# A linear-attention and mixture-of-experts kernel: ScalarE's order in the first steps, an earlier load of the experts' first rows, and the last tile scaled by two engines

## The chip, the cores and the metric

The kernel runs on one core of a Trainium2 chip. The core has five engines with their own instruction queues: TensorE (PE, matmuls; PEld are its weight loads), VectorE (DVE), ScalarE (ACT), GpSimd (POOL) and SyncE (SP, which here only issues DMA transfers). They run in parallel and meet at semaphores. The metric is the device time of one execution in microseconds (us), the median of several.

## The reference, cut to what matters

```python
f = 1.0 / (1.0 + np.exp(-f_logit))              # batch 4, heads 8, seq 768, head_dim 48
for t in range(S):
    state = f[:, :, t, :, None] * state + np.einsum('bhd,bhe->bhde', k[:, :, t], v[:, :, t])
    y[:, :, t] = np.einsum('bhd,bhde->bhe', q[:, :, t], state)
x = y.transpose(0, 2, 1, 3).reshape(B * S, H * D)   # 3072 tokens of 384 numbers
logits = x @ w_gate                              # 8 experts
expert_idx = np.argmax(logits, axis=1)
gate_w = softmax(logits)[expert_idx]
h = np.maximum(x_of_expert @ w1[e], 0.0)         # 384 -> 1024
y = h @ w2[e]                                    # 1024 -> 384
out = gate_w[:, None] * y
```

First a gated linear attention, then a layer in which each token goes to the one expert with the largest logit. How many tokens an expert gets is known only when all tokens have been through the attention.

## The kernel before, in words

**First half, attention in units.** The sequence is cut into 6 chunks of 128 tokens and the batch into two pairs, which gives 12 units (`NU`). The recurrence inside a unit becomes matmuls: with the running sum of log f, keys are multiplied by its exponential (`growth`, `by_r`) and queries by its inverse (`decay`, `by_decay`). For each unit, `steps` and `log` compute exp and log of f on ScalarE, `total` is VectorE's running sum, `score` is q times k (PE s), `mask` copies the causal half out of PSUM (VectorE, 4 per unit), `keys` transposes k on TensorE into PSUM (kp) and `keep` copies it to SBUF on ScalarE (kn), `within` and `before` make the output (PE yt), `added` and `update` make the new state (PE dp), `settle` copies yt to ys on ScalarE. `rows` turns ys into token rows and logits by matmuls (PE xp), and `lay` copies these rows out of PSUM on ScalarE into xr. `turns` gives out two PSUM buffers in turn to kp, xp, dp and a few others, so dp of a step needs the buffer of the first xp, which has to be copied out by `lay` before.

**The order.** It is written out by hand: the loop over `n` from 1 to 13 (`NU + 1`) issues the instructions of step n for units n+3 to n-2, and every engine executes its own in this order. Unit n's scores, unit n-1's outputs and unit n-2's rows fall into step n. `settle(last)` stands at the head of a step and copies unit n-2's output. There is one yt buffer in PSUM and one ys buffer in SBUF.

**Routing.** When a group of units (0 and 1, 2 and 3, ... , 10, 11) has its rows, `choose` (six small VectorE operations) finds each token's expert, `count` ranks the tokens by two matmuls, `place` turns this into a row of the DRAM buffer `xs`, `fill` writes the gate weight, and `send` scatters the rows by indirect DMA from GpSimd (L183), 128 tokens per scatter, 24 in all. Up to units 4 and 5 a step sends two scatters; later groups send all of theirs at once. The scatters are declared not to depend on each other, but a load from xs waits for all scatters ahead of it in the program, and a scatter behind a load waits until the load has landed.

**Early experts.** Experts 0 and 1 (`EARLY`) start before all tokens are placed. Their first 128 rows are loaded at the end of step 11:

```python
            if n == NU - 1:
                soon = [load_rows(first[e]) for e in range(EARLY)]
```

Each `load_rows` is four transfers of 48 KB and one small one (tg: token and gate). VectorE transposes them (`turn`), and TensorE widens them (L304 into s) in between the last attention steps, then narrows them (L320 into yp). In `settled`, three tiny VectorE operations (L716 to L720) test whether these experts have 128 rows at the time when they are loaded; if not, a slow path at the end repairs it. Weights of experts 0 and 1 (two tensors of 1.5 MB each) are loaded at the ends of steps 8 and 10.

**Second half, the experts.** For each expert, in tiles of up to 384 rows: `widen` (PE hps, L304), relu on ScalarE and VectorE in turn, `narrow` (PE yps, L320) for each 128 rows, and `put`: VectorE multiplies by the gate weight (L331) and GpSimd scatters the rows into the output.

Of the kernel before, what the change touches and what calls it, by code (L numbers as in the profile page):

```python
# [10 lines left out]
F32 = mybir.dt.float32  # L11
# [108 lines left out]
def kernel(  # L120
# [194 lines left out]
                else:  # L315
                    nc.vector.tensor_scalar(to, x["h"], 0.0, None, op0=OP.max)  # L316

    def narrow(x, t, w, yp, group="out"):
        for f in range(NF):
            nc.tensor.matmul(  # L320
                yp,
                lhsT=x["hT"][:, f, t * C : t * C + C],
                rhs=w[1][:, f, :],
                start=f == 0,
                stop=f == NF - 1,
            )
        put(x, t, yp, group)

    def put(x, t, yp, group):
        ysb = ep.tile([128, DM], F32, name="ysb")  # L330
        nc.vector.tensor_scalar(ysb, yp, x["tg"][:, t, 1:2], None, op0=OP.mult)  # L331
        scatter(out, x["dst"][:, t : t + 1], ysb, N - 1, group)


# [48 lines left out]
    with ExitStack() as st:  # L383
# [92 lines left out]
        def ends(u):  # L476
            nc.gpsimd.tensor_copy(rend[:, u], units[u]["sum"][:, :, C])

        def decay(u, part=whole):
            x = units[u]  # L480
            x["dec"] = x["g"][:, :, 1:CR]
            nc.scalar.activation(
                x["dec"][:, part], x["sum"][:, part, 1:CR], AF.Exp, scale=-1.0
            )
# [223 lines left out]
        def settled(n, rt):  # L708

            rt.place()  # L710
            rt.fill()
            lead["base"] = rt.after
            if n == NU - 3:
                lack = wk.tile([1, EARLY], F32, name="lack", bufs=1)
                some = wk.tile([1, 1], F32, name="some", bufs=1)
                nc.vector.tensor_tensor(  # L716
                    lack, rt.after[0:1, 0:EARLY], const("full")[0:1, 0:EARLY], op=OP.is_lt
                )
                nc.vector.reduce_max(some, lack, axis=AX_X)
                nc.vector.tensor_copy(fix, some)  # L720
            if n < NU:
                for c in range(0, rt.n, 2):
                    sends.append(lambda c=c: rt.send(range(c, c + 2)))
            else:
                rt.send(range(rt.n))
# [3 lines left out]
        def scatter_some(n):  # L729
            now = sends if n >= NU - 1 else sends[:1]  # L730
            for send in now:
                send()
            del sends[: len(now)]
# [31 lines left out]
        for n in range(1, NU + 2):  # L765
            here, back, last = n, n - 1, n - 2
            ahead = n + 1 < NU
            state = n < NU - 2
            rt = None
            if here < NU:  # L770
                units[here]["old"] = states[here % 2]
            if 1 <= last:
                settle(last)
            if later and later[0] < NU - 1:
                later[1].weigh()
            if here < NU:
                for a in range(2):
                    score(here, a)
            if ahead and n != 2:
                by_r(n + 1)  # L780
                ends(n + 1)
            if decayed:
                decayed()
                decayed = None
            if sends:
                scatter_some(n)
            if n == 1:
                units[0]["old"] = None
                added(0)
                update(0)()  # L790
            if ahead and n != 2:
                decay(n + 1)
                last_decay(n + 1)
            if state:
                keys(here)
                keep(here)
            if n == 2:
                growth(n + 1)
                by_r(n + 1)
                ends(n + 1)  # L800
                decay(n + 1)
                last_decay(n + 1)
            if here < NU:
                for a in range(2):
                    for h in range(2):
                        mask(here, a, h)
            if n == 1:
                log(3)
            if n + 3 < NU:
                steps(n + 3)  # L810
            if later and n >= NU - 1:
                settled(*later)
                later = None
                scatter_some(NU)
            if 2 < n < NU - 2:
                total(n + 2)
            if n == NU - 2:
                by_decay(n + 1)
            if 0 <= last:
                rt = rows(last, later[1] if later else None)  # L820
                lay(last)
            if later and n == NU - 2:
                settled(*later)
                later = None
                scatter_some(NU)
            if ahead and n < NU - 2:
                by_decay(n + 1)
            if n == 2:
                total(n + 2)
            if rt:  # L830
                rt.choose()
                if n < NU - 2:
                    routed.append(rt.latest)
                if n >= NU - 1:
                    rt.weigh()
            if later:
                settled(*later)
                routed.append(later[1].latest)
                later = None
            for a in range(2):  # L840
                if back < NU:
                    within(back, a)
            if n == 1:
                settle(0)
            if n + 2 < NU and n != 1:
                growth(n + 2)
            if n == NU + 1:
                widen(soon[0], weights[0], early_h, range(3, 7))
            if n == NU:
                turn_early(soon[0])  # L850
            if state:
                added(here)
                decayed = update(here)
            if n == 1:
                total(3)
            if back < NU:
                before(back)
            if rt:
                later = (n, rt)
                if n >= NU - 1:  # L860
                    rt.count(turns("rp", [128, 2, rt.n, E]))
                if n >= NU:
                    settled(*later)
                    later = None
            if n == NU:
                early_h = early_banks()
                widen(soon[0], weights[0], early_h, range(3))
            if n == NU + 1:
                widen(soon[0], weights[0], early_h, range(7, NF))
                turn(soon[1])  # L870
            if n == 1:
                load(n + 3, "q")
            if n + 3 < NU:
                load(n + 3, "k")
            if n + 2 < NU:
                load(n + 2, "v")
            if 1 < n and n + 3 < NU:
                load(n + 3, "q")
            if n + 5 < NU:
                load(n + 5, "f")  # L880
            if n == 1:
                load_first_pads()
            if n in (8, 10):
                load_first_weights((n - 8) // 2)
                load_second_weights((n - 8) // 2)
            if n == NU - 1:
                soon = [load_rows(first[e]) for e in range(EARLY)]


        def share():  # L890
# [91 lines left out]
    def tile_pools(st):  # L982
        pool = lambda name, bufs: st.enter_context(tc.tile_pool(name=name, bufs=bufs, space=PSUM))
        psh, psz = pool("psh", 6), pool("psz", 2)

        def bank(i):
            return psh.tile([128, 512], F32, name="hps")

        def narrow_late(x, t, w, group="out"):
            narrow(x, t, w, psz.tile([128, DM], F32, name="yps"), group)  # L990

        return bank, narrow_late, psz

    with ExitStack() as st:
# [86 lines left out]
        for e in range(E):  # L1081
            x, w = rows_of[e], weights[e]
            x["hT"] = qp.tile([128, NF, TILES * C], F32, name="hT")[:, :, 0 : x["n"] * C]
            widen(x, w, bank, range(NF))
            if e in WITH:
                widen_quad(quad)
            if e + 1 < E:
                turn(rows_of[e + 1])
            if e + 1 in WITH:
                turn(quad, qp)  # L1090
            if e + 2 < E:
                rows_of[e + 2] = load_expert(e + 2)
                load_first_weights(e + 2)
            fetch(2 * e)
            if e in WITH:
                turn_quad(quad)
            for t in range(x["n"]):
                if e in WITH and t == 2:
                    narrow_quad(quad)
                narrow_late(x, t, w)  # L1100
            if e + 2 < E:
                load_second_weights(e + 2)
            fetch(2 * e + 1)
# [155 lines left out]
```

## Time and profile before

| | us |
|---|---|
| time, median of 3 | 409.92 |
| lowest and highest | 407.5, 410.32 |
| span of the profiled execution | 410.9 |
| TensorE busy | 390.1 |
| VectorE, GpSimd, ScalarE busy | 170.6, 112.3, 102.9 |

A line of the profile names the engine, the source line, the operation, the output and its inputs, and a count. An idle time in brackets stands before an instruction with the work that ended it; "issue" means that the profile shows nothing it waited for, and "remote" a semaphore whose sender is not in the records. The chain of work that ended last is followed back from the last instruction, at each step to what released it. The attention ends near 127 us; the experts fill the rest.

### The profile page before, as it was taken

Reading aid. Unit: us, or ns where it says so; the run is one execution under the profiler, and the core shown is the slowest. Engines: PE = TensorE matmul, PEld = TensorE weight load, DVE = VectorE, ACT = ScalarE, POOL = GpSimd, SP = SyncE. Lnnn points to the kernel's source line nnn. Section 1 sums busy time; section 2 is a strip of 40 time slices with the busy share of each in tenths; the row PEclk is TensorE's granted clock in tenths of the full one; section 3 lists DMA queues with packets and bytes.
Section 4 is the critical chain, followed back from the end, with each engine's and each line's share of the span. In section 5 each row is a group of like instructions: output and inputs, shape, how many; then the busy total and the mean of one; then the engine's idle time right before and its main releaser. Section 6 shows DMA issues by size and latency. Waiting matters only on the chain.

```text
span 410.9 us, 7299 instructions
## 1 busy us (share of the span) xinstructions
PE 390.1 (95%) x2870; PEld 272.1 (66%) x2870; DVE 170.6 (42%) x364; ACT 102.9 (25%) x190; POOL 112.3 (27%) x118
## 2 busy tenths in 40 slices
PE   7878999999999699999999999999999999999991
PEld 7878899989978478685555555545455555554540
DVE  6989888887752631212131131119112113111810
ACT  7888778675232001010100100110000000001000
POOL 5378667778705200000001001000200100100020
PEclk9998999999999699999999999999999999999997
DMA  8998667769953358785539999892172379994010
GB/s 291 406 359 296 213 213 256 237 200 360 404 156 105 121 157 282 176 294 109 185 108 396 362 384 332 322 352 31 51 255 83 97 252 383 405 406 169 1 46 17
DMA packets 52122, 95.22 MB, mean 232 GB/s; under 512 B 21440, under 2 KB 41333, under 8 KB 50032
## 3 DMA queue, kind: packets, MB, share of 16 engines
q1 hardware_dynamic: 48592, 84.96, 61.1%
q0 software_dynamic: 3200, 9.64, 6.3%
q8 instruction: 24, 0.39, 0.4%
q10 hardware_dynamic: 288, 0.08, 0.1%
q14 instruction: 18, 0.15, 0.1%
HBM read 79.65 MB, written 15.40 MB: 231 GB/s over the span
## 4 chain that ended last, share of the span: by engine, by line
PE 86%; DMA 4%; ACT 3%; DVE 2%; another core or an unknown queue 1%; issue 1%; SPq 0%; POOL 0%; POOLq 0%; ACTq 0%; DVEq 0%
PE yps L320 28%; PE hps L304 28%; PE xp L625 6%; PE yt L533 5%; PE s L505 4%; DMA f<-in_fu_dram 4%; PE yp L320 3%; PE yps L1059 3%; PE hps L1033 3%; PE yt L554 2%; PE s L304 2%; PE dp L570 2%; PE kp L520 1%; ACT g L438 1%
## 5 line engine op out<-in xcount | busy, mean ns | idle before, releaser
L320 PE MATMUL yps<-w2t,hT 128*128 128x384 f32 x352 | 115.6, 487 | 0.0
L304 PE MATMUL hps<-xT,w1t 128*128 128x384 f32 (+1 forms) x384 | 114.9, 459 | 0.0
L304 PEld LDWEIGHTS hps<-xT,w1t 128*128 128x128 f32 x384 | 73.0, 190 | 41.1
L320 PEld LDWEIGHTS yps<-w2t,hT 128*128 128x128 f32 x352 | 66.5, 190 | 48.1 <-issue 2.9
L183 POOL DMA_INDIRECT out_dram<-ysb,dst x26 | 25.3, 972 | 239.7 <-DVE ysb L331 239.4
L314 ACT ACTIVATE hT<-hps 128x384 f32<-128x384 f32 (+1 forms) x28 | 14.1, 505 | 209.7 <-PE hps L304 190.8
L316 DVE TENSOR_SCALAR hT<-hps 128x384 f32<-128x384 f32 (+1 forms) x28 | 16.2, 577 | 97.2 <-PE hps L304 97.2
L331 DVE TENSOR_SCALAR ysb<-yps,tg 128x384 f32<-128x384 f32 x22 | 13.6, 618 | 73.4 <-PE yps L320 73.4
L183 POOL DMA_INDIRECT xs<-xr,posi x24 | 30.9, 1289 | 22.3 <-issue 16.7
L511 DVE COPY_PREDICATED at<-mpack,s 128x512 f32<-128x512 uint8 x48 | 31.2, 727 | 11.9 <-PE s L505 10.3
L471 POOL TENSOR_TENSOR k<-k,r 128x1024 f32<-128x1024 f32 (+1 forms) x12 | 26.5, 2209 | 25.6 <-ACT r L467 9.9
L625 PE MATMUL xp<-fpack,ys 128*128 128x104 f32 x192 | 25.9, 286 | 4.6 <-ACT kn L525 3.7
L453 DVE TENSOR_TENSOR_SCAN sum<-g,cap 128x1032 f32<-128x1032 f32 (+1 forms) x14 | 28.7, 2051 | 2.7 <-ACT g L446 2.6
L625 PEld LDWEIGHTS xp<-fpack,ys 128*128 128x128 f32 x192 | 23.3, 196 | 6.9 <-ACT kn L525 4.9
L505 PE MATMUL s<-q,k 64*128 64x128 f32 x384 | 24.7, 278 | 1.6 <-POOL last L489 1.0
L533 PE MATMUL yt<-at,v 128*48 128x128 f32 x384 | 25.1, 282 | 0.6 <-issue 0.6
L505 PEld LDWEIGHTS s<-q,k 64*128 64x128 f32 x384 | 22.4, 188 | 3.5 <-issue 1.5
L533 PEld LDWEIGHTS yt<-at,v 128*48 128x48 f32 x384 | 21.3, 127 | 2.6 <-issue 1.6
L320 PE MATMUL yp<-w2t,hT 128*128 128x384 f32 x32 | 13.6, 584 | 3.3 <-DVE hT L316 3.3
L494 DVE TENSOR_TENSOR q<-q,g 128x1024 f32<-128x1024 f32 (+1 forms) x14 | 16.4, 1182 | 0.0
L595 ACT COPY ys<-yt 128x512 f32<-128x512 f32 x24 | 12.8, 587 | 13.8 <-PE yt L554 13.8
L288 DVE STREAM_TRANSPOSE xT<-xrow 128x1152 f32<-128x1152 f32 (+2 forms) x10 | 14.3, 1433 | 0.8 <-DMA xrow<-xs 0.7
(110 smaller groups left out, 324.6 us busy)
## 6 DMA issues: line engine op xcount, KB each, us to landing
qw<-in_moe_w_dram SPq DMA_DIRECT2D x16, 1536.0 KB
w1t<-in_moe_w_dram SPq DMA_DIRECT2D x8, 1536.0 KB
w2t<-in_moe_w_dram SPq DMA_DIRECT2D x8, 1536.0 KB
k<-in_ku_dram SPq DMA_DIRECT2D x12, 512.0 KB
q<-in_qu_dram SPq DMA_DIRECT2D x12, 512.0 KB
f<-in_fu_dram SPq DMA_DIRECT2D x11, 512.0 KB
xs<-pad SPq DMA_DIRECT2D x8, 600.0 KB
v<-in_vu_dram SPq DMA_DIRECT2D x12, 384.0 KB
```

Of the source, the lines that this page charges most:

```text
L183: ins = nc.gpsimd.indirect_dma_start(out=dst, out_offset=bass.IndirectOffsetOnAxis(ap=idx, axis=0), in_=src, in_offset=None, bounds_check= ...
L288: nc.vector.transpose(x["xT"].rearrange("p k (i c) -> p i k c", c=BK), x["x"].rearrange("p i (r k) -> p i k r", k=KD),)
L304: nc.tensor.matmul(x["h"][:, f], lhsT=w[0][:, j, b * 128 : b * 128 + 128], rhs=x["xT"][:, j], start=j == 0, stop=j == KD - 1,)
L316: nc.vector.tensor_scalar(to, x["h"], 0.0, None, op0=OP.max)
L320: nc.tensor.matmul(yp, lhsT=x["hT"][:, f, t * C : t * C + C], rhs=w[1][:, f, :], start=f == 0, stop=f == NF - 1,)
L453: nc.vector.tensor_tensor_scan(x["sum"][:, part].rearrange("p s c -> p (s c)"), x["g"][:, part].rearrange("p s c -> p (s c)"), cap[:, part ...
L471: ins = on.tensor_tensor(k, k, units[u]["r"][:, part], op=OP.mult).ins
L494: nc.vector.tensor_tensor(q, q, x["dec"][:, part], op=OP.mult)
L505: nc.tensor.matmul(ps[h][:, p], lhsT=x["k"][r, s], rhs=x["q"][r, s], start=True, stop=True)
L511: nc.vector.copy_predicated(x["at"][:, a, h], _bc(causal, 1, HP), x["ps", a][h])
L533: nc.tensor.matmul(x["yt"][DP * (h ^ a) : DP * (h ^ a) + D, a, p], lhsT=x["v"][:, a, 2 * p + h], rhs=x["at"][:, a, h, p], start=p == 0, st ...
L625: nc.tensor.matmul(xp[:, p], lhsT=x["ys"][:, a, p], rhs=wx[:, p, 0:XW] if a else wx[:, p, E:WX], start=True, stop=True,)
```

## The change

Three edits, each meant to take a wait off TensorE's path. (1) In steps 1 to 3 ScalarE's copies that TensorE waits for (ys, kn) are issued ahead of exponentials that nobody waits for at that time. Unit 0's and unit 1's ys are copied in the step that computes them; unit 4's decay goes behind unit 3's kn. (2) The first rows of experts 0 and 1 are loaded in step 10 and not at the end of step 11; they then come from the tokens of units 0 to 5, and the test for 128 rows moves two groups ahead. (3) The scaling of the very last tile is divided by columns between VectorE and ScalarE.

```diff
-    def narrow(x, t, w, yp, group="out"):
+    def narrow(x, t, w, yp, group="out", last=False):
...
-        nc.vector.tensor_scalar(ysb, yp, x["tg"][:, t, 1:2], None, op0=OP.mult)
+        gate, half = x["tg"][:, t, 1:2], DM // 2 if last else 0
+        nc.vector.tensor_scalar(ysb[:, half:], yp[:, half:], gate, None, op0=OP.mult)
+        if last:
+            nc.scalar.activation(ysb[:, 0:half], yp[:, 0:half], AF.Copy, scale=gate)
...
-            if n == NU - 3:
+            if n == NU - 5:
                 lack = wk.tile([1, EARLY], F32, name="lack", bufs=1)
...
-            if 1 <= last:
+            if 2 <= last:
                 settle(last)
...
             if sends:
                 scatter_some(n)
+            if n == NU - 2:
+                soon = [load_rows(first[e]) for e in range(EARLY)]
...
-            if ahead and n != 2:
+            if ahead and not 1 < n < 4:
                 decay(n + 1)
                 last_decay(n + 1)
...
                 ends(n + 1)
+            if 1 < n < 4:
                 decay(n + 1)
                 last_decay(n + 1)
...
             if n == 1:
                 log(3)
+                within(0, 0)
+                within(0, 1)
+                settle(0)
             if n + 3 < NU:
                 steps(n + 3)
...
-                if back < NU:
+                if 0 < back < NU:
                     within(back, a)
-            if n == 1:
-                settle(0)
+            if n == 2:
+                settle(1)
...
-            if n == NU - 1:
-                soon = [load_rows(first[e]) for e in range(EARLY)]
...
-                narrow_late(x, t, w)
+                narrow_late(x, t, w, last=e == E - 1 and t == x["n"] - 1)
```

On TensorE the order of instructions is unchanged. On VectorE only the three small test operations move and the last scaling is halved; on ScalarE the order changes as told and one instruction is added; on the DMA queue the ten transfers of the rows go ahead of expert 1's two weights; GpSimd's order is unchanged.

More of the change, by code (lines that the diff above doesn't have):

```diff
@@ L326, in narrow, with put @@
             )
-        put(x, t, yp, group)
-    def put(x, t, yp, group):
+        put(x, t, yp, group, last)
+    def put(x, t, yp, group, last=False):
         ysb = ep.tile([128, DM], F32, name="ysb")
-        nc.vector.tensor_scalar(ysb, yp, x["tg"][:, t, 1:2], None, op0=OP.mult)
+        gate, half = x["tg"][:, t, 1:2], DM // 2 if last else 0
+        nc.vector.tensor_scalar(ysb[:, half:], yp[:, half:], gate, None, op0=OP.mult)
+        if last:
+            nc.scalar.activation(ysb[:, 0:half], yp[:, 0:half], AF.Copy, scale=gate)
         scatter(out, x["dst"][:, t : t + 1], ysb, N - 1, group)
@@ L987, in bank, with narrow_late @@
             return psh.tile([128, 512], F32, name="hps")
-        def narrow_late(x, t, w, group="out"):
-            narrow(x, t, w, psz.tile([128, DM], F32, name="yps"), group)
+        def narrow_late(x, t, w, group="out", last=False):
+            narrow(x, t, w, psz.tile([128, DM], F32, name="yps"), group, last)
         return bank, narrow_late, psz
```

## The prediction

> **What bounds the kernel now.** I read first the chain of work that ended last, in order of time, to find where TensorE is not the link. TensorE carries 86% of that chain, and from 41.7 us to the end it is nearly unbroken, so an edit pays only at the places where the chain leaves TensorE.
>
> ```profile
> 27.31 0.72 ACT ys L595 x2
> 28.25 0.61 ACT kn L525
> 28.90 2.74 PE xp L625 x16
> ...
> 38.15 0.26 ACT g L482
> 38.99 0.59 ACT kn L525
> 39.63 2.03 PE xp L625 x16
> ...
> 128.47 6.06 another core or an unknown queue
> ...
> 136.07 0.67 DVE hT L316
> 136.78 5.49 PE yp L320 x8
> ...
> 402.39 0.63 DVE ysb L331
> ```
>
> Columns: start, duration, what. There are three places. Early, TensorE's xp matmuls of units 0 and 1 wait for ScalarE's kn copy, and ahead of kn stands ys (27.31), then a decay (38.15). Near 128 the chain sits 6.06 us in something that has no name in it. At the end, the scaling by VectorE stands alone, with TensorE finished.
>
> Then I read the instructions in order of time from 118 to 137 us, to put names to the second place. In brackets is the idle time before an instruction and what ended it.
>
> ```profile
> 118.35 1.76 SPq L267 DMA_DIRECT2D xrow<-xs  x4
> 125.89 0.97 POOL L183 DMA_INDIRECT xs<-xr,posi  x1 [11.81 <-issue]
> 132.51 0.97 POOL L183 DMA_INDIRECT xs<-xr,posi  x1 [0.31 <-issue]
> 134.56 0.17 DVE L228 COPY counts<-rp 128x16 f32<-128x16 f32 x1 [6.08 <-remote]
> 136.78 5.49 PE L320 MATMUL yp<-w2t,hT 128*128 128x384 f32 x8 [3.35 <-DVE hT L316]
> ```
>
> The experts' first rows are read from xs by loads issued from 118.35; GpSimd's next scatter into xs stands still for 11.81 us, until those loads have landed; six scatters then follow back to back until 133.48; VectorE's counts copy, whose matmul input ended near 130.1, starts only at 134.56, and TensorE pays 3.35 us. The first eight yp matmuls before the gap took 2.75 us, the eight after it 5.49. That is the half clock, which the table by stage shows:
>
> ```profile
> core 0: us, PE busy (x) PEld busy (x) DVE busy (x) ACT busy (x) POOL busy (x), PEclk, DMA share, GB/s
> ...
> 28.90:35.30 6.40, 6.40 (x82) 6.14 (x82) 4.36 (x5) 5.24 (x9) 4.93 (x3) 0.73 0.83 303
> ...
> 136.80:142.30 5.50, 5.50 (x10) 3.08 (x11) 4.15 (x19) 0.00 (x0) 2.02 (x2) 0.50 0.54 186
> ```
>
> Granted clock is 0.50 after the 3.35 us gap, and 0.73 after the early gap of 1.70 us (27.20 to 28.90).
>
> [...] scatters into xs take 2.6 us from issue to landing at the least and 6.1 at the most, the slow ones while expert 1's weights stream at about 400 GB/s (100 to 116 us). [...] the scatter at 96.68 beside a scan takes 2.31 us, the one at 95.33 takes 1.05.
>
> **Part 1, ScalarE's order.** No instruction is added or removed. (a) Unit 0's two ys copies (1.05 us) go ahead of the exponential of unit 4, which waits until 25.16 for its f to land. Their input, the yt matmuls, ended at 22.66, so they fit into 23.3 to 24.4, inside ScalarE's wait of 1.87 us: free. kn of unit 2 then starts at 27.31 instead of 28.25; minus 0.94 for xp. TensorE's gap becomes about 0.75 us, so I expect the half clock of 30 to 33.5 not to come (xp 2.73 back to 2.03, yt 2.86 back to 1.95). (b) Unit 1's ys goes one step earlier, ahead of the growth of unit 4, which waits 1.96 us for VectorE's scan anyway: free. (c) kn of unit 3 goes ahead of unit 4's decay, so it starts when TensorE has transposed the first half of the keys. TensorE waited 1.28 us there. Worked forward: xp of unit 0 at 27.95, yt to 31.9; then dp needs ScalarE's copy of the first xp out of PSUM (33.27 before, about 32.7 now, 0.48 long), so dp starts at 33.2 and gives back 1.2; scores of unit 3 at 34.2, kn 36.8, xp of unit 1 at 37.4 against 39.63. In the next step the same copy (after kn 1.07, decay 1.06, exp 1.09+0.2, log 1.06) ends near 41.7, and scores of unit 4 start at 43.7 against 45.41. After that each step is TensorE's own length, so 1.7 us stays. Bounds: 0.9 (only part a) and 2.2 (xp's own gain). Unit 4's decay comes about a microsecond later relative to kn; behind it is VectorE's product for q, needed at 43.7 and ready at 42.8, so it is hidden.
>
> **Part 2, the rows' loads.** Ten loads move from the end of step 11 to step 10, ahead of expert 1's weights in the queue, and ahead of units 6 and 7's four scatters. The test that experts 0 and 1 have 128 rows moves two groups earlier: three VectorE operations of 0.12 to 0.14 us, same number. The loads now wait for units 4 and 5's scatters, issued at 104.30 and 105.64. With the weights behind them those land about 2.6 us after issue: 108.2. From first load to the release of GpSimd took 125.89 - 118.35 = 7.5 us, so the rows are there at 115.7. What is queued behind the new wait: on the DMA queue the two weights (1.5 MB each), which start near 113 instead of 99.9; at 400 GB/s they need 8 us, while their user starts at 142.3: hidden. On GpSimd the four scatters at 109.27 move to 115.7. Then all ten run at 1.28 us each: 115.7 + 10 x 1.28 = 128.5, instead of 133.5. Minus part 1's 1.7, and minus what 109 to 116 loses now (TensorE busy 6.40 of 7.00, with masks of VectorE late by 1.0 and 0.7 us beside the same four scatters; about 1.3 us up to 116.9), both shift together. So the last counts copy, due at 130.1, comes after the ten scatters instead of among them. Removed: 3.35 us of waiting and 5.49 - 2.75 = 2.74 us of half clock, 6.1 in all, and 1.3 near 112. Added: the same interference, now in 116 to 128. The trace has no such ten in a row. From below: VectorE's choice of experts, beside scatters at 127.3 to 128.4, ran at its usual 0.2 us per operation, cost 0. From above: it costs what it cost before, 7.4. I take two bursts of four at 1.3, 2.7, because the choice of experts and the ys copies have 1 to 2 us of TensorE work beside them. Net 7.4 - 2.7 = 4.7. The profiled execution took 412.75 us against the median of 409.92, so some 2.8 us of this may belong to the profile; I take off half, 1.4: 3.3.
>
> **Part 3, the last tile.** VectorE's 0.62 us for 384 columns becomes 192 columns beside ScalarE's 192. Differences in the trace (512 columns 0.69, 384 columns 0.62, and 0.56 for the plain maximum) leave a fixed part near 0.3, so 0.35 to 0.45 is my estimate; ScalarE's copy of 192 columns takes 0.33. [...] Gain 0.2.
>
> Sum: 1.7 + 3.3 + 0.2 = 5.2; 409.9 - 5.2 = 404.7.
>
> **Rivals.** A (0.53), as worked: 404.7, spread 401 to 407; the lower end has all of part 2 (4.7), the half clock gone early and 2.2 from part 1. B (0.30), the wait moves: ten scatters in a row delay the choice of experts or ys within steps 11 to 13, another gap of 3 us with its half clock comes there, and only parts 1 and 3 remain: 409.9 - 1.9 = 408.0. For it: the counts copy was let go only when the last scatter had ended. Against: at 126 to 128.4 VectorE ran freely beside scatters. C (0.11), part 1 is eaten too, since dp waits for ScalarE's xp copies, now queued behind more work, and another mostly idle stretch brings the half clock again: about 409.7. D (0.06), slower: the ten scatters meet expert 1's weights, as the four at 109 do (TensorE lost 1.3), each four cost more, and two gaps with half clock come instead of one: 409.9 - 1.9 + 6.1 = 414.1.
>
> **How the numbers follow.** 1% is 4.1 us, the bound 405.8. Some three quarters of A lie below it, and of B nearly a fifth, if the wait comes back only in part: 0.41 + 0.06; I add 0.05 because A's lower end is open (the trace charges 7.4 us to the stretch that part 2 rearranges): 0.52. Within 1%: 0.42. Slower: 0.06, from D. The range, 401.0 to 409.6, holds A and B and leaves out D, most of C and A's far end.
>
> **What would show it.** Right: the row loads issue near 106, the long idle time of GpSimd's scatter stands before units 6 and 7's and ends near 114; ten scatters end before 128; no counts copy waits several microseconds; the granted clock stays 1.00 from 130 to 142; early, ys before 25 and xp of unit 1 near 37.5; the last scaling ends 0.4 after TensorE. Wrong: if the unnamed wait turns up again between 114 and 128 with TensorE idle behind it (B, D), if dp in steps 2 and 3 waits for the xp copies by more than 1.2 us (C), or if the row loads wait longer than 108, because units 4 and 5's scatters still land slowly behind expert 0's weights.

## The result and the profile after

The changed kernel took 403.9 us (median of 4, 403.55 to 404.59), the kernel before 410.12 beside it (407.5 to 410.57): ratio 0.986, interval 0.982 to 0.990. The forecast was 404.7 us, in a range of 401.0 to 409.6. The number came out; of the reason behind its largest term, part 2, only half did, as the experiments show. Medians here are over all executions, ratios only over those that do not count as slow (on chip B below this leaves out ten of the 60 of the kernel before and none of the others), so the two do not divide exactly.

First the early steps, in order of time (start, duration, engine and line; in brackets the idle time before and what ended it). Line numbers are three higher than before in the attention (L525 is now L528) and seven higher in the experts' part.

```profile
27.89 1.05 ACT L528 COPY kn<-kp 128x512 f32<-128x512 f32 x2
...
29.36 2.00 PE L628 MATMUL xp<-fpack,ys 128*128 128x104 f32 x16 [1.73 <-DMA fpack<-in_moe_w_gate_dram]
...
33.39 1.14 PE L573 MATMUL dp<-v,kn 128*64 128x48 f32 x32 [0.15 <-ACT xr L658]
...
37.14 1.07 ACT L528 COPY kn<-kp 128x512 f32<-128x512 f32 x2 [0.34 <-PE kp L523]
37.78 2.03 PE L628 MATMUL xp<-fpack,ys 128*128 128x104 f32 x16 [0.24 <-ACT kn L528]
...
44.15 1.05 PE L508 MATMUL s<-q,k 64*128 64x128 f32 x14
```

The first half of kn of unit 2 is done near 28.5, yet xp starts at 29.36: the last thing it waits for is the gate weights (the transfer of w_gate into fpack), which hid behind kn before. Of the second wait 0.24 us is left: xp of unit 1 starts at 37.78 instead of 39.63.

Then the stretch round the rows' loads.

```profile
107.63 1.76 SPq L267 DMA_DIRECT2D xrow<-xs  x4
...
115.33 0.99 POOL L183 DMA_INDIRECT xs<-xr,posi  x1 [9.10 <-DVE counts L228]
...
127.08 0.97 POOL L183 DMA_INDIRECT xs<-xr,posi  x1 [0.30 <-ACT ex L248]
...
127.52 0.17 DVE L228 COPY counts<-rp 128x16 f32<-128x16 f32 x1 [1.66 <-PE rp L221]
...
128.08 5.33 PE L320 MATMUL yp<-w2t,hT 128*128 128x384 f32 x16
```

GpSimd stands still for 9.10 us until the rows are there (the last of them issue at 112.67; these loads land 1.8 to 3.5 us after issue), then ten scatters run to 128.05. The last counts copy follows its matmul at once, and all sixteen yp matmuls run in one piece in 5.33 us; before it was 2.75, a gap of 3.35 and 5.49. The table by stage (columns as in the prediction) says the same, with TensorE busy 13.00 of 13.00 and the clock at 1.00 everywhere:

```profile
28.90:35.30 6.40, 5.79 (x94) 5.42 (x96) 5.05 (x6) 5.82 (x11) 5.32 (x3) 1.00 0.98 335
116.00:129.00 13.00, 13.00 (x149) 12.19 (x149) 6.43 (x40) 3.83 (x11) 9.59 (x14) 1.00 0.97 361
136.80:142.30 5.50, 5.50 (x31) 4.12 (x30) 2.24 (x8) 0.00 (x0) 0.00 (x0) 1.00 0.59 159
```

Last, the end:

```profile
393.27 0.42 DVE L332 TENSOR_SCALAR ysb<-yps,tg 128x192 f32<-128x192 f32 x1 [4.71 <-PE yps L320]
393.72 0.42 ACT L334 ACTIVATE ysb<-yps,tg 128x192 f32<-128x192 f32 x1 [23.57 <-DVE ysb L332]
394.42 0.97 POOL L183 DMA_INDIRECT out_dram<-ysb,dst  x1 [4.61 <-ACT ysb L334]
```

VectorE's half costs 0.42, within the estimate of 0.35 to 0.45, and ScalarE's as much; but ScalarE starts when VectorE has ended: from the start of the scaling to the scatter 1.15 us, against 0.90 before.

### The profile page after: what moved, and what is told of

Read it like the earlier page. It is cut to its first block, busy times and chain, and to the rows that moved or that the text cites. A ratio compares the mean times of both kernels' runs of the same rounds, so it can differ in the third digit from the quotient of the medians.

```text
span 402.0 us, 7302 instructions
## 1 busy us (share of the span) xinstructions
PE 385.5 (96%) x2870; PEld 269.5 (67%) x2870; DVE 169.9 (42%) x364; ACT 103.4 (26%) x191; POOL 114.5 (28%) x118
## 5 line engine op out<-in xcount | busy, mean ns | idle before, releaser
L320 PE MATMUL yps<-w2t,hT 128*128 128x384 f32 x352 | 115.6, 487 | 0.0
L320 PEld LDWEIGHTS yps<-w2t,hT 128*128 128x128 f32 x352 | 66.5, 190 | 48.1 <-issue 2.9
L314 ACT ACTIVATE hT<-hps 128x384 f32<-128x384 f32 (+1 forms) x28 | 14.2, 506 | 209.7 <-PE hps L304 199.5
L332 DVE TENSOR_SCALAR ysb<-yps,tg 128x384 f32<-128x384 f32 (+1 forms) x22 | 13.4, 609 | 73.4 <-PE yps L320 73.4
L536 PE MATMUL yt<-at,v 128*48 128x128 f32 x384 | 23.5, 275 | 0.0
L536 PEld LDWEIGHTS yt<-at,v 128*48 128x48 f32 x384 | 20.4, 123 | 1.3 <-issue 0.2
L598 ACT COPY ys<-yt 128x512 f32<-128x512 f32 x24 | 12.9, 591 | 14.2 <-PE yt L557 14.2
L1060 DVE STREAM_TRANSPOSE hqT<-hq 32x256 f32<-32x256 f32 x32 | 13.9, 436 | 0.5
## 6 DMA issues: line engine op xcount, KB each, us to landing
w2t<-in_moe_w_dram SPq DMA_DIRECT2D x8, 1536.0 KB, 14.2
```

The costliest lines, as they stand in the source:

```text
L320: nc.tensor.matmul(yp, lhsT=x["hT"][:, f, t * C : t * C + C], rhs=w[1][:, f, :], start=f == 0, stop=f == NF - 1,)
L536: nc.tensor.matmul(x["yt"][DP * (h ^ a) : DP * (h ^ a) + D, a, p], lhsT=x["v"][:, a, 2 * p + h], rhs=x["at"][:, a, h, p], start=p == 0, st ...
```

## The experiments

The four sets of runs fell on three chips, here A, B and C. That turned out to be the point, so the table has it. "Holes" are idle times of TensorE near 112 to 139 us for which the trace shows no waiting reason, or waits for a VectorE step that itself starts late after its matmul.

| kernel | chip | us, median | to before beside it | holes |
|---|---|---|---|---|
| part 1 alone | B | 410.4 | 0.9946 (0.9921 to 0.9970) | yes |
| part 2 alone | B | 415.5 | 1.0105 (1.0075 to 1.0134) | yes |
| parts 1 and 2 | B | 413.3 | 1.0059 (1.0039 to 1.0079) | yes |
| gap filled | B | 411.7 | 0.9980 (0.9955 to 1.0006) | yes |
| changed | A | 403.8 | 0.9861 (0.9828 to 0.9893) | no |
| part 3 alone | A | 410.4 | 1.0006 (0.9985 to 1.0027) | no |
| parts 1 and 2, weights early | A | 403.5 | 0.9849 (0.9817 to 0.9881) | no |
| part 1 alone | C | 407.1 | 0.9943 (0.9919 to 0.9966) | yes |
| part 2 alone | C | 415.3 | 1.0129 (1.0085 to 1.0172) | yes |
| parts 1 and 2, gate weights early | C | 418.3 | 1.0200 (1.0156 to 1.0245) | yes |
| changed | A | 403.5 | 0.9857 (0.9819 to 0.9894) | no |
| parts 1 and 2 | A | 403.3 | 0.9854 (0.9815 to 0.9892) | no |

The kernel before took 412.1 us on B, 409.2 and 410.3 on A, 409.3 on C. The chip of the first two traces, before and after, is not on record; the first has holes and the second none.

The last column tells of one traced execution each, and two of these are not typical of their rows. Part 3 alone on A was traced at 409.1 us with a granted clock of 0.992; 12 of its 14 executions had a lower one, and so had 21 of the 30 of the kernel before on A, down to 0.981, the clock of the first trace with its holes. Part 1 alone on C was traced at 409.9 us, its third slowest of 22.

### The parts one by one, on chip B

Part 1 alone is the diff's six edits in the order of work; part 2 alone is this; the third kernel has both and the old scaling.

```diff
-            if n == NU - 3:
+            if n == NU - 5:
...
+            if n == NU - 2:
+                soon = [load_rows(first[e]) for e in range(EARLY)]
...
-            if n == NU - 1:
-                soon = [load_rows(first[e]) for e in range(EARLY)]
```

> The kernel before with ScalarE's new order alone. Theory 'sum of independent parts': the traces of before and after part by 1.7 us (net of the later start) by unit 4's scores and by nothing more up to 109 us, so this kernel shows scores of unit 4 near 44.1 and a time 1.7 us under the kernel before (408.4); the 3.35 us gap and the half clock behind it stay. Rival 'the phase decides': the unnamed wait near 130 depends on which work meets which scatter, so 1.7 us of shift are enough to make it vanish or grow; then the time differs by 6 us more (about 402, or 414). Rival 'eaten': at most 0.5 us remain at the end.

> The kernel before with the experts' first rows loaded in step 10, nothing else. Theory 'sum of independent parts': the whole difference that the profiles show from 109 us on (7.9 us of the 9.1) is this edit's; profiled span down by about 7.5, scatters back to back from about 117 to 130, no gap of TensorE over 1 us near 130 and clock 1.00 there; timed gain 4.5 (6.2 less 1.7). Rival 'needs both': without the 1.7 us of part 1 the counts copy meets the last scatters and a gap of 2 to 3 us with a half clock comes; timed gain 0 to 2.

> The changed kernel with the last tile scaled by VectorE alone, in one piece. Theory: the two halves ran one after the other (ScalarE started 0.45 us after VectorE, at its end), so from the start of the scaling to the scatter's issue it was 1.15 us against 0.90; undone, the end comes 0.25 us after the changed kernel's, ahead of it: span 0.25 lower, time 403.6 against 403.9, a difference that is hardly measurable as time but is to be read from the last rows. Rival: the wait of ScalarE is an artefact of the record and the halves cost nothing: the scatter follows TensorE's end as in the changed kernel.

Part 1 won 0.54% (2.2 us); in its trace unit 4's scores start at 43.65, though the first xp waits 2.0 us for the gate weights (in the trace of part 2 alone, which has the old order there, at 46.15), and the gap before the second eight yp matmuls is still there, 2.47 us. Part 2 lost 1.05%, and both together lost 0.59% (0.3% by the medians), about the sum of the two; no expectation of these runs had part 2 losing. So on this chip the change without part 3 is slower than before, 9.4 us above the 403.9 of the changed kernel, from which it differs only in the last microsecond. The trace of the two parts together shows where, in order of time:

```profile
118.35 0.42 PE L554 MATMUL yt<-q,state 48*48 48x128 f32 x4
...
119.65 0.27 PE L554 MATMUL yt<-q,state 48*48 48x128 f32 x1 [0.34 <-issue]
120.35 0.42 PE L554 MATMUL yt<-q,state 48*48 48x128 f32 x4 [0.43 <-issue]
121.08 0.27 PE L554 MATMUL yt<-q,state 48*48 48x128 f32 x1 [0.31 <-issue]
...
126.06 0.80 PE L554 MATMUL yt<-q,state 48*48 48x128 f32 x9 [0.77 <-issue]
...
127.66 4.19 PE L304 MATMUL s<-xT,w1t 128*128 128x128 f32 x18
```

The 32 small matmuls of unit 11, which need 1.09 us, start in bursts of one to nine, with nothing named that they wait for ("issue"), from 118.35 to 126.86. The half clock follows (granted 0.53 from 121 to 131 us): the next eighteen matmuls take 4.19 us instead of 2.25.

### The gap filled, on chip B

```diff
+            if f == 3 and fill:
+                fill()
...
-        narrow_early(soon[0], weights[0])
+        narrow_early(soon[0], weights[0], lambda: warm(13))
```

> The kernel before with 13 small matmuls without use (0.236 us each, 3.1 us in all, into a PSUM buffer that is no longer read) in TensorE's queue where it stood idle for 3.35 us near 133.4. No other work moves. Theory 'the half clock is a price of the gap': the wait stays, but the eight yp matmuls behind it take 2.75 us instead of 5.49 at clock 1.00, and the profiled span is 2.7 us shorter; in timed runs 1.3 to 2.7 if the gap is there too. Rival 'the gap belongs to the profile': timed executions have no gap there, so 13 more matmuls cost up to 3.1 us. Rival 'the slow eight have another cause': they stay at 5.5.

```profile
134.58 2.95 PE L672 MATMUL yt<-pad 128*128 128x128 f32 x25
138.46 0.27 PE L672 MATMUL yt<-pad 128*128 128x128 f32 x1 [0.93 <-issue]
139.19 0.48 PE L320 MATMUL yp<-w2t,hT 128*128 128x384 f32 x1 [0.46 <-DVE slot L929]
139.90 2.51 PE L320 MATMUL yp<-w2t,hT 128*128 128x384 f32 x7 [0.23 <-issue]
```

The eight yp matmuls behind the filled gap (L320, the last two rows) take 2.99 us at clock 1.00 instead of 5.49: in this trace, the half clock was a price of the gap. But the fill itself met a hole, so the stretch from 134.58 to the first of these matmuls lasted 4.6 us, and the time was not measurably better (0.998). The other end of the expectation, up to 3.1 us lost, did not come either.

### Chip or program

> The changed kernel once more, unaltered, beside the kernel before. Without part 3 alone it took 413.3 us (1.006 of the kernel before), with it 403.9 (0.986), though part 3 touches only the last microsecond. Theory 'the chip or the execution decides': TensorE's standing still at 118 to 127 us comes and goes with the place of execution, so the unaltered kernel now takes 412 to 414 too and its trace shows the same holes in unit 11's yt matmuls. Rival 'the program decides': 403.5 to 404.6 again, no holes; then the two instructions at the end move something 270 us ahead of them.

> The changed kernel, unaltered, a third time, beside the changed kernel without part 3 on the same chip. So far the changed kernel took 403.8 twice (one chip known), and the kernel without part 3 413.3, on another chip. Theory 'the chip decides': both take the same within 0.5 us here, 404 if TensorE has no holes in unit 11's yt matmuls on this chip, 412 to 414 if it has. Rival 'the program decides': this one takes 404 and has no holes, and the one without part 3 takes 413 with holes, on one and the same chip.

> The changed kernel without part 3 a second time, beside the changed kernel. Theory 'the chip decides': as the changed kernel on this chip, less 0.25 us. Rival 'the program decides': 413 with holes at 118 to 127 us while the changed kernel takes 404 without them.

The second and third of these ran on one chip, A, and took 403.5 and 403.3. The kernel without part 3, the very same one, took 413.3 on B and 403.3 on A; beside the kernel before on the same chip the ratios are 1.0059 and 0.9854, with intervals far apart. All 22 executions on B lie above 412.3 and all six on A below 404.8. The chip (or what goes with it) decides, not part 3; each kernel had one set of runs on B, so chip and moment are not separated. The same rows on A:

```profile
118.22 1.09 PE L554 MATMUL yt<-q,state 48*48 48x128 f32 x32
...
119.71 2.25 PE L304 MATMUL s<-xT,w1t 128*128 128x128 f32 x18
```

### Part 3 alone, and what the kernel before waits for on chip A

> The kernel before with the last tile scaled in two halves, nothing else. Theory 'two readers of one PSUM tile run one after the other': the end comes 0.25 us later, ratio 1.000 to 1.001. Rival 'the program decides': the same two instructions that parted 413.3 from 403.9 take several microseconds off here too, ratio 0.98 to 0.985.

No measurable difference (1.0006). On A, the end of the kernel without part 3 shows what the halves cost:

```profile
392.57 0.62 DVE L331 TENSOR_SCALAR ysb<-yps,tg 128x384 f32<-128x384 f32 x1 [4.71 <-PE yps L320]
...
393.46 0.97 POOL L183 DMA_INDIRECT out_dram<-ysb,dst  x1 [4.36 <-DVE ysb L331]
```

0.89 us from scaling to scatter in one piece, 1.15 in halves (393.77 minus 392.62 in the changed kernel beside it). The medians, 403.3 and 403.5, agree but don't part by themselves.

Up to its last microsecond the kernel with part 3 alone is the kernel before, and its trace is the only one of that order on chip A. In order of time:

```profile
118.58 1.76 SPq L267 DMA_DIRECT2D xrow<-xs  x4
...
123.29 0.69 DVE L288 STREAM_TRANSPOSE xT<-xrow 128x384 f32<-128x384 f32 x1 [3.63 <-DMA xrow<-xs]
...
124.03 3.82 PE L304 MATMUL s<-xT,w1t 128*128 128x128 f32 x18 [2.27 <-DVE xT L288]
...
127.69 1.93 PE L628 MATMUL xp<-fpack,ys 128*128 128x104 f32 x16
...
132.71 0.17 DVE L228 COPY counts<-rp 128x16 f32<-128x16 f32 x1 [1.54 <-PE rp L221]
```

No late counts copy (1.54, its usual wait), no gap at 133. Here the loads themselves are late: issued at 118.58, they land at 123.3; VectorE waits 3.63 us for the rows, TensorE 2.27 for the transposed rows, and the eighteen matmuls behind take 3.82 us instead of 2.25, at a granted clock of 0.83 from 121 to 131 us (1.00 in the last trace of the changed kernel).

### Part 2 and part 1 alone, on chip C

> The kernel before with the rows' loads moved alone, once more, because the first look at it fell on a chip where TensorE stood still in holes of its own, and the changed kernel's two looks did not. Theory 'two chips, two waits': on a chip without these holes the kernel before loses 2.3 us near 122 where the early experts' first matmul waits for the transposed rows, and 1.7 us of half clock behind it; this edit takes both away, ratio 0.990 (409.2 to 405.2), and 1.013 again on a chip with holes. Rival 'needs part 1': the ratio is 0.996 or more even without holes.

> The kernel before with ScalarE's new order alone, once more, beside the other half of the change. Theory 'sum of independent parts': scores of unit 4 1.6 us earlier than in the kernel before, and the rest shifts with it, ratio 0.996 (409.2 to 407.6) on a chip without holes; with the other part it makes up the 5.4 us of the whole. Rival 'eaten': the rows' loads wait for units 6 and 7's scatters, not for TensorE, so 1.6 us earlier on TensorE only lengthens the wait for the transposed rows from 2.3 to 3.9 us, and the ratio is 1.000.

All traces on C have holes as on B, and the ratios repeat: 1.0129 and 0.9943. The 1.6 us that were expected early do not show in the trace of part 1: behind a wait of 1.8 us for the gate weights the half clock came there (0.79 from 28 to 36 us), and unit 4's scores start at 45.20, against 45.60 in part 2 alone. Neither part was timed alone on A, without holes; there part 2 stands only as the difference of the whole and a part 1 that was measured elsewhere.

### Two variants

> The changed kernel without part 3, with expert 1's two weights (1.5 MB each) loaded at the end of step 9 and not after the rows' loads at the end of step 10, so that the ten scatters no longer run beside them. Theory 'scatters beside a full DMA stream hold TensorE up': the 3.6 us of standing still at 118 to 127 and the half clock there go away, about 5 to 8 us less than 413.3 (405 to 408). Rival 'ten scatters in a row are enough': the holes stay, 412 to 414. Rival 'the stream only moves': units 4 and 5's scatters land later, the rows too, and the whole is 2 to 4 us slower.

```diff
-            if n in (8, 10):
-                load_first_weights((n - 8) // 2)
+            if n in (8, 9):
+                load_first_weights(n - 8)
```

(and the same for the second weights.) It ran on A, where there are no holes to take away, so it says nothing on them. 403.5 against 403.3 and 403.5: with the scatters from 120.55 to 133.26 instead of 115.33 to 128.05 TensorE loses nothing either.

> The changed kernel without part 3, with the four small loads of the gate weights (6 KB each) issued right after the constants and ahead of four loads of units 2 to 5. In the changed kernel the first xp waits 0.6 to 1.7 us for them (28.65 to 29.36 instead of 27.95). Theory: that wait goes away, xp of unit 0 starts near 28.0, and 0.4 to 1 us are won at the end, unless dp of step 2 gives it back by waiting for ScalarE's copy of xp; with part 3's 0.25, 402.7 to 403.3 on a chip without holes (about 412.5 on one with). Rival: the four loads ahead delay k of unit 3 and f of unit 4 by as much as they win, 403.5; or the dp wait takes the whole gain, 403.5.

```diff
         load_consts()
+        load_gate()
         load(3, "k")
...
-        load_gate()
```

It fell on C and was 2.0% slower than before. Parts 1 and 2 without it were not timed on C; their two ratios there multiply to about 1.007, so some 1.3% of it, an estimate, is the moved load's. Queue, ScalarE and TensorE in order of time:

```profile
22.60 2.59 SPq L174 DMA_DIRECT2D fpack<-in_moe_w_gate_dram  x4
...
25.78 0.38 SPq L428 DMA_DIRECT2D f<-in_fu_dram  x1
```

```profile
30.03 1.06 ACT L438 ACTIVATE g<-f 128x1024 f32<-128x1024 f32 x1 [4.94 <-DMA f<-in_fu_dram]
```

```profile
32.80 3.74 PE L625 MATMUL xp<-fpack,ys 128*128 128x104 f32 x16 [4.77 <-ACT kn L525]
```

The gate weights go into the same buffer as the constants, so their issue stood at the head of the queue from about 15.6 to 22.60, until the constants had landed (in the kernel before and in the changed one the same issue waits 3.2 and 3.4 us for that landing), and behind it unit 4's f, which otherwise issues at 16.11 (parts 1 and 2 on B). ScalarE waited 4.94 us for f, with kn behind it, and xp started at 32.80 instead of 28.81 (parts 1 and 2 on A). Here a wait at the head of the queue was the wait of all behind it; the expectation had only the length of the four transfers.

## Why the prediction was right, and where it was not

**Part 1 (1.7 us, bounds 0.9 and 2.2).** The size agrees. On A, unit 4's scores start at 45.35 in the order before (part 3 alone, first below) and at 43.51 in the last run of the changed kernel: 1.84, of which 0.25 is an earlier start, so 1.6.

```profile
29.70 2.00 PE L628 MATMUL xp<-fpack,ys 128*128 128x104 f32 x16 [1.85 <-DMA fpack<-in_moe_w_gate_dram]
...
39.57 2.03 PE L628 MATMUL xp<-fpack,ys 128*128 128x104 f32 x16 [1.70 <-ACT kn L528]
...
45.35 2.06 PE L508 MATMUL s<-q,k 64*128 64x128 f32 x32
```

```profile
28.74 2.00 PE L628 MATMUL xp<-fpack,ys 128*128 128x104 f32 x16 [1.13 <-DMA fpack<-in_moe_w_gate_dram]
...
37.13 2.03 PE L628 MATMUL xp<-fpack,ys 128*128 128x104 f32 x16 [0.24 <-ACT kn L528]
...
43.51 2.06 PE L508 MATMUL s<-q,k 64*128 64x128 f32 x32
```

Alone it was worth 0.54% and 0.57%, 2.2 and 2.3 us (intervals 1.2 to 3.3). Step (a) as such failed: xp of unit 0 was to start at 27.95 and started at 28.65 to 29.36 in the three traces of the changed kernel, since kn hid a second wait, that for the gate weights. The order before on A waits 1.85 us for them at that place too, so there (a) shows no kn wait removed. That xp starts 0.96 earlier in this pair is an earlier landing of these weights, issued at 22.47 and 22.44; that the new order brought it about is not shown. Steps (b) and (c) give the other 0.9 us of the pair, and some 2.4 on B, where xp of unit 0 starts alike in the old and the new order (29.62 in part 2 alone and 29.57 in part 1 alone) and unit 4's scores do not (46.15 and 43.65). In the first trace dp, unit 3's scores, kn and xp of unit 1 were forecast for 33.2, 34.2, 36.8 and 37.4 and came at 33.39, 34.46, 37.14 and 37.78, all late by 0.2 to 0.4 only: dp waits for ScalarE's xp copy, as forecast, and so the late xp of unit 0 did not carry on. That wait was at most 0.65 us, so rival C is out.

**Part 2 (net 4.7, after the discount 3.3).** As a sequence it came: loads at 107.63 (106.5 forecast), ten scatters to 128.05 (126.8), no late counts copy, clock 1.00. The size, 4.7 before the discount, came roughly: in the same two traces on A the first early-expert matmul moves from 124.03 to 119.76, 1.84 of it by the shift of part 1; the 2.43 left are the wait for the rows and a little more. The next xp moves from 127.69 to 121.85, another 1.57 of half clock (3.82 less 2.25). 2.4 + 1.6 = 4.0 us, and with part 1's 1.8 that is the 5.8 by which the spans part (407.2 and 401.4). In the changed kernel:

```profile
119.76 2.25 PE L304 MATMUL s<-xT,w1t 128*128 128x128 f32 x18
121.85 1.93 PE L628 MATMUL xp<-fpack,ys 128*128 128x104 f32 x16
```

What failed is what was to be removed: 3.35 us of waiting with 2.74 us of half clock, and 1.3 near 112. Those are the holes of the one trace I had; in the one trace of the old order on A they are absent, and a wait that the first trace hid, the rows' landing, stands in their place (3.63 us for the transposition, against 0.74 in the first trace). Most executions of the kernel before on A had a lower clock than that trace, so holes in some of them are not excluded; what those executions waited for was not traced.

**The term added (2.7, bounds 0 and 7.4) and the rivals.** Without holes it was 0. With them part 2 costs 1.05% and 1.29%: the wait is not removed, it moves to unit 11's yt, 118 to 127 us, into the stretch that rivals B and D named, and costs more there than before. Whether it comes by the road of rival B (a late choice of experts or ys) or of rival D (expert 1's weights) was not shown. Rival D, worked at 414.1 or 4.2 over the kernel before, had a chance of 0.06; parts 1 and 2 took 413.3 on B, 1.2 over it by the medians. The forecast gave one number to two cases that lie 10 us apart, and it named the wrong thing to tell them by: which kernel, not which chip.

**The discount of 1.4.** It took the 2.8 us between the profiled execution and the median for a cost of the profile. No run bears that out: the changed kernel's profiled execution (403.87) is about its median, others lie below theirs (408.7 against 410.4, part 1 on B) or above, and the kernel before scatters from 406.6 to 414.5 over the three chips.

**Part 3 (0.2).** VectorE's price was right (0.42 in 0.35 to 0.45), ScalarE's half took 0.42 against the 0.33 of its plain copy of 192 columns, and the overlap was wrong: the halves run one after the other, 0.26 us lost instead of 0.2 won.

**The sum.** That it met the measured time so closely is in part luck. In the pair on A 4.0 us were removed and not 7.4, nothing was added where 2.7 were priced, the discount of 1.4 had no ground, and part 3 lost a little; these errors nearly cancel. And the result fell where the changed kernel had no holes; on B parts 1 and 2 took 413.3, outside the range.

**Open.** What makes the holes. In the traces of a known chip they come on B and C and not on A. In those of part 2, parts 1 and 2 and the filled gap on B they begin while GpSimd's scatters follow each other every 1.28 us or so, at the fourth or later of a row; in that of parts 1 and 2 on B, TensorE starts again about every 0.72 us (119.65, 120.35, 121.08, 121.78). In all eight traces with holes the experts' second weights (w2t) have no landing time, in all six without they have one (14.2 to 16.0 us from issue, the median), so records are missing with the holes. The traced execution on B (412.9) was no slower than the median of its row (413.3), so the holes are not confined to the execution that is read as a trace. What joins the missing records and the standing still, and whether the scatters bring on either, no run here shows; scatters held back on a chip with holes were not tried.

## What to carry to other kernels

A wait that the trace ends with "remote" or "issue" names no owner in the program: look for it in a second trace, best from another chip, before an edit is priced on it, and price the wait that stands behind it as well. A change of order that moves a burst of transfers is to be timed on more than one chip; here the same kernel was 1.5% faster than before on one and 0.6% slower on another (0.3% by the medians). Before a transfer is moved ahead in a queue, ask what it waits for: here the loads behind the moved one waited as well, unit 4's f until 25.78 instead of 16.11.

## What was not expected of the hardware

- The same program, 403.3 us on one chip and 413.3 on another, the kernel before 409 to 412 on all three.
- On A the kernel before spreads over 406.6 to 412.0 us, the changed one over 403.3 to 404.3. That the wait that was removed is also the one that varied would fit this; it is not shown, with one trace of the old order there.
- An idle time of one length has different prices. TensorE waited 1.73 us (changed kernel), 1.85 and 1.70 (order before, on A) and 2.0 (part 2 alone, on B) in the early steps at clock 1.00; behind 1.70 in the kernel before and 1.8 in part 1 alone on C the half clock came (0.73 from 28.9 to 35.3, 0.79 from 28 to 36), and a lower clock also behind 1.8 on A in the variant with the weights early (0.94 over 30 to 60 us, as in part 1 alone on C; 1.00 there in the changed kernel). The forecast of no half clock behind a gap of 0.75 us was an estimate from one gap of 1.70 that had it. The length of the gap alone does not decide here; what else does, these runs do not separate.
- VectorE and ScalarE, reading two halves of one PSUM tile and writing two halves of one SBUF tile, ran one after the other in the first and the last trace of the changed kernel: 0.42, then a start at 393.72 after 393.27 (393.08 after 392.62 in the last), 0.42.
